# Three chained layers on one core: token blocks of 384 in place of 288, and scores and masks of the first attention pairs formed another way

## The chip, the cores and the metric

One core of a Trainium2 chip runs the kernel. TensorE multiplies matrices into the eight banks of PSUM (b0 to b7), VectorE, ScalarE and GpSimd work element by element, and SyncE (SP) issues the transfers. The metric is the device time of one execution in microseconds.

## The reference

```python
# q, k, v: (4, 8, 576, 64), f: (4, 8, 576)
scores = q @ k^T / 8;  cum = cumsum(log(clip(f, 1e-4, 1)))
scores = where(causal, -1e9, scores + cum[:, None] - cum[None, :])
attn = exp(scores - max) / (sum + 1e-9);  x = attn @ v       # -> (2304 tokens, 512)
h = ((x @ w1) * (x @ w2)) @ w3 @ w_out                       # 512 -> 1024 -> 1024 -> 512
h2 = h @ w_in;  out = (h2 - tanh(h2)) @ w_out2               # 512 -> 2048 -> 512
```

There are 32 heads (4 batches of 8) and 2304 tokens, 576 in a batch.

## The kernel before

**Arithmetic.** A float32 matrix is split into a high part in float32r and the rest, and a product is three float32r products (high by high, high by low, low by high; `mm3`, lines 202 to 205). A weight tile of 128x512 is loaded as 64-bit words into a buffer `w64`, cut to 32 bits by one ScalarE instruction (L279) and four VectorE instructions (L269, L271, L273, L275; `conv`), and split by ScalarE (L289) and GpSimd (L292). A load (L264) waits until VectorE has released a buffer. There are three such buffers (`NW`).

**Attention.** A pair p is two heads (y = 0, 1) of batch p // 4. `head` loads q and k twice, once to the upper and once to the lower 64 partitions (L309), and the row of decays to all partitions (`cumb`, L313). ScalarE casts both (L314, L315: KH, QH), VectorE subtracts (L316: the low part of q in the lower half of QH; L318: KL), and the scores are two float32r products, QH by KH and QH by KL (L325), for pieces of 512, 512, 384, 64, 256 and 128 columns. GpSimd adds the causal mask `tri` (-1e30 above the diagonal) onto the decay row's diagonal block (L331), five times per head. VectorE adds scores and decays, scales them and takes the minimum (L340), ScalarE takes the exponential (L345), TensorE transposes by 128x128 blocks (L386), ScalarE copies them out (L389). The product with the values (`pvm`, L430, and `pvt`, L436) is in float32, 64 output rows per head. The row sums go out and come back by transfer (`dr`, `rb`), and VectorE scales the result into the tile `xy` (L439, L440).

**Layers.** `mphase` forms w3 by w_out once (M, 192 products of 512 columns). `block1` takes 288 tokens through the first layer: the x of the block is cast and subtracted (L482, L483), 16 groups of 12 products with w1 and w2, an elementwise product (L499 to L503), 8 groups of 12 products with M, and the result goes to DRAM (`yd`). A second loop takes the same blocks through the second layer: 16 times 12 products with w_in, eleven elementwise instructions (L601 to L612), 12 products with w_out2. `xy` exists twice, for even and odd batches; blocks 2b and 2b+1 are of batch b.

**Order.** `Plan` collects all operations with engine, estimated length, keys that are read and written, and a due time, and sorts each engine's instructions by a list schedule over these. The due times are lines of the table `PR` with the constants `C`: `att(p)` for pair p (a0, a1 for the first four, a2, a3 for the others), `wo`, `w3`, `w12` for the weight tiles, `m` for M, `blk(t)` for blocks. An engine then runs its list strictly in that order.

## Time and profile before

| | us |
|---|---|
| median of 3 runs (lowest, highest) | 1019.44 (1016.18, 1020.94) |
| the profiled execution | 1024.94 |
| its span from the first to the last instruction | 1023.2 |
| TensorE busy | 950.8 (93%) |
| VectorE busy | 740.0 (72%) |
| ScalarE busy | 604.6 (59%) |
| GpSimd busy | 325.3 (32%) |

The granted TensorE clock is 0.987 on average. Busy time is the share of the span in which an engine has an instruction under way; matmuls overlap one another, so a product's own duration is longer than the distance between two starts.

### The profile page before, as it was taken

How to read it: one execution, taken by the hardware profiler on the slowest of the kernel's cores; microseconds unless marked ns; L12 is line 12 of the kernel's file. 1: busy time of each engine (PE TensorE's matmuls, PEld its weight loads, DVE VectorE, ACT ScalarE, POOL GpSimd, SP SyncE). 2: the span in 40 equal slices, each digit the busy share in tenths (PEclk: the TensorE clock that was granted, in tenths of full speed). 3: DMA queues.
4: the chain of work that ended last, by engine and by line, in shares of the span. 5: the costliest groups of instructions: out<-in, count | busy, mean ns of one | idle time of the engine just before them, and what ended most of it. 6: DMA issues, size and time to landing. Idle time of an engine off the chain costs nothing.

```text
span 1023.2 us, 19522 instructions
## 1 busy us (share of the span) xinstructions
PE 950.8 (93%) x6944; PEld 889.1 (87%) x6944; DVE 740.0 (72%) x1681; ACT 604.6 (59%) x1532; POOL 325.3 (32%) x398
## 2 busy tenths in 40 slices
PE   1788885889999999999999999999999999999998
PEld 1466664778988988899999999999999999999998
DVE  6888898976887868544633238887777777777785
ACT  4766556655656656545422357766666666666674
POOL 1544444431121121110310358424242424242221
PEclk9989999899999999999999999999999999999999
DMA  8556745556677676420410243000000000000000
GB/s 248 168 174 186 199 154 187 151 150 210 200 214 220 186 221 197 117 73 19 137 45 1 76 134 113 24 25 24 24 25 24 24 24 1 24 1 25 1 25 24
DMA packets 46114, 104.25 MB, mean 102 GB/s; under 512 B 5888, under 2 KB 18304, under 8 KB 46016
## 3 DMA queue, kind: packets, MB, share of 16 engines
q1 hardware_dynamic: 46016, 103.01, 33.7%
q8 instruction: 54, 0.88, 0.4%
q14 instruction: 44, 0.36, 0.1%
HBM read 87.11 MB, written 15.88 MB: 101 GB/s over the span
## 4 chain that ended last, share of the span: by engine, by line
PE 65%; DMA 14%; DVE 10%; ACT 6%; issue 3%; SPq 2%; POOL 1%; DVEq 0%; ACTq 0%; POOLq 0%
PE b L205 20%; PE b L204 20%; PE b L203 20%; DMA rb<-dr 5%; DMA spo<-w 3%; PE b L386 2%; DMA cumb<-cumd 2%; PE b L325 2%; DVE w L273 2%; DVE w L275 2%; ACT P L345 1%; DVE w L271 1%; DMA dr<-rt 1%; DVE KL L318 1%; DVE P L340 1%
## 5 line engine op out<-in xcount | busy, mean ns | idle before, releaser
L612 POOL TENSOR_TENSOR gl<-w,gl 128x288 fp32r<-128x288 f32 x120 | 102.5, 854 | 233.6 <-ACT gl L611 230.8
L331 POOL TENSOR_TENSOR cumb<-cumb,tri 128x128 f32<-128x128 f32 (+1 forms) x160 | 89.6, 563 | 272.7 <-DVE MX L340 167.8
L608 ACT ACTIVATE fa<-fa,cb 128x288 f32<-128x288 f32 x128 | 68.6, 536 | 61.2 <-DVE w L607 60.9
L603 DVE SCALAR_TENSOR_TENSOR w<-b,fa 128x288 f32<-128x288 f32 x128 | 57.9, 452 | 60.9 <-ACT fb L602 59.5
L325 PE MATMUL b<-KH,QH 128*64 128x512 f32 (+3 forms) x192 | 68.5, 365 | 32.5 <-DVE MX L340 20.8
L345 ACT ACTIVATE P<-P,MX 128x512 f32<-128x512 f32 (+3 forms) x128 | 71.9, 562 | 23.8 <-DVE MX L340 23.4
L610 DVE COPY_PREDICATED w<-fa,fb 128x288 f32<-128x288 uint32 x128 | 70.0, 547 | 18.9 <-ACT fa L608 10.7
L386 PE MATMUL b<-idf,P 128*128 128x128 f32 x320 | 56.6, 294 | 29.2 <-DVE xy L439 18.2
L607 DVE SCALAR_TENSOR_TENSOR w<-fa,w 128x288 f32<-128x288 f32 x128 | 83.1, 649 | 0.1
L340 DVE CUSTOM_DVE_ANT_0 P<-b,cumb 128x512 f32<-128x512 f32 (+3 forms) x128 | 62.0, 485 | 27.2 <-POOL cumb L331 22.6
L389 ACT COPY PT<-b 128x512 f32<-128x512 f32 (+3 forms) x128 | 51.1, 425 | 51.2 <-PE b L386 49.4
L601 ACT ACTIVATE fa<-b 128x288 f32<-128x288 f32 x128 | 52.5, 410 | 43.1 <-PE b L205 42.9
L386 PEld LDWEIGHTS b<-idf,P 128*128 128x128 f32 x320 | 40.1, 148 | 38.8 <-DVE xy L439 11.2
L325 PEld LDWEIGHTS b<-KH,QH 128*128 128x128 f32 (+1 forms) x192 | 35.0, 182 | 43.5 <-DVE MX L340 26.8
L500 DVE TENSOR_TENSOR fb<-b,fa 128x288 f32<-128x288 f32 x64 | 29.0, 454 | 59.4 <-PE b L205 57.5
L605 ACT ACTIVATE w<-fa,cb 128x288 f32<-128x288 f32 x128 | 69.2, 541 | 0.0
L611 ACT CAST gl<-w 128x288 fp32r<-128x288 f32 x120 | 51.9, 433 | 26.5 <-DVE w L610 26.2
L279 ACT ACTIVATE w<-w 128x512 f32<-128x512 f32 x72 | 48.7, 678 | 31.7 <-DMA spo<-w 8.4
L325 PE MATMUL b<-KL,QH 128*64 128x512 f32 (+3 forms) x192 | 56.9, 336 | 1.1 <-DVE KL L318 1.1
L606 DVE TENSOR_TENSOR fb<-b,fb 128x288 f32<-128x288 f32 x128 | 57.1, 446 | 1.0 <-ACT fb L602 1.0
L273 DVE SCALAR_TENSOR_TENSOR w<-w,w 128x512 uint32<-128x512 uint32 x72 | 55.5, 775 | 0.7
L275 DVE SCALAR_TENSOR_TENSOR w<-w,w 128x512 uint32<-128x512 uint32 x72 | 53.3, 743 | 0.4
(842 smaller groups left out, 3674.1 us busy)
## 6 DMA issues: line engine op xcount, KB each, us to landing
qk<-in_qk_dram SPq DMA_DIRECT2D x64, 288.0 KB
w<-in_wo_dram SPq DMA_DIRECT2D x24, 512.0 KB
cumb<-cumd SPq DMA_DIRECT2D x32, 288.0 KB
w<-in_w3t_dram SPq DMA_DIRECT2D x16, 512.0 KB
...
```

The lines of the kernel that those rows point to most:

```text
L203: E.matmul(o, lh, rh, start=start, stop=False)
L204: E.matmul(o, lh, rl, start=False, stop=False)
L205: E.matmul(o, ll, rh, start=False, stop=stop)
L273: V.scalar_tensor_tensor(m, s[:, :, 1], 0xC0000000, m, ALU.bitwise_and, ALU.bitwise_or)
L275: V.scalar_tensor_tensor(m, s[:, :, 0], 29, m, ALU.logical_shift_right, ALU.bitwise_or)
L325: E.matmul(T[p][0:qn, at:at + c1 - c0], T["QH"][:, 128 * i:128 * i + qn], T[k][:, c0:c1], start=z == 0, stop=z == 1)
L331: G.tensor_tensor(t, t, T["tri"][0:qn, 0:qn], op=ALU.add)
L340: V.tensor_tensor_reduce(out=out, in0=T[p][0:qn, at:at + c1 - c0], in1=T[cum][0:qn, c0:c1], scale=-0.125, scalar=3e38, op0=ALU.add, op1=AL ...
L345: A.activation(t, t, AF.Exp, bias=T["MX"][:, z:z + 1], scale=-1.0, accum_out=T["SM"][:, z:z + 1])
L386: E.transpose(T["b2"][0:n, 128 * z:128 * z + 128], T[src][:, c:c + n], T["idf"])
L607: op("D", d_dve(NB), lambda w=w, u=u: V.scalar_tensor_tensor(T[w], T[u], -P_ROOT, T[w], ALU.add, ALU.mult), r=[u], w=[w], lk=True, **pa)
L612: op("P", d_pool(NB), lambda w=w, gh=gh, gl=gl: G.tensor_sub(T[gl], T[w], T[gh]), r=[w, gh], w=[gl], **pa)
```

## The change

The token block `NB` grows from 288 to 384, so there are 6 blocks in place of 8; three blocks are two batches, and the blocks 1 and 4 reach over the end of a batch. `xy` becomes one tile of two batches' columns with keys for its thirds, `yd` one tensor. The order of declaration is pairs 0 to 3, pairs 4 to 7 with blocks 0 and 1, pairs 8 to 11 with block 2, pairs 12 to 15 with blocks 3 to 5.

For the first five pairs (`nf`) a head's scores are one float32 product of q and k as loaded, over 128 partitions of which the lower 64 are set to zero once; casts, subtractions and the second load are left out. For the first nine pairs (`nm`) the mask is a further small float32r product, an identity (`idr`) by `tri`, added in the same bank; GpSimd's five additions are left out.

The probability tiles P exist once in place of twice, the weight buffers `w64` twice in place of three times, and two scratch tiles come from elsewhere. The constants of the due times all change. The diff, without some lines of the same kind:

```diff
@@ -19,7 +19,7 @@
...
 DM, FF1, FF2 = 512, 1024, 2048
-NB = 288
+NB = 384
 NBLK = NT // NB
...
@@ -35,7 +35,7 @@
...
-C = {"a0": 3.76, "a1": 20.5, "a2": 108.54, "a3": 38.68, "o0": 2.46, "o1": 5.33, "w0": 29.91, "w1": 5.05, "m0": 71.33, "v0": 91.92, "v1": 5.1, "s0": 1170.31, "s1": 10.17, "lod": 2, "evd": 7, "b0": 1619.63, "k0": 1007.92}
+C = {"nf": 5, "nm": 9, "a0": 4.99, "a1": 16.68, "a2": 100.35, "a3": 35.07, "o0": 1.62, "o1": 5.79, "w0": 24.48, "w1": 6.0, "m0": 138.47, "v0": 144.48, "v1": 5.72, "s0": 1192.89, "s1": 8.9, "lod": 1, "evd": 9, "b0": 2090.17, "k0": 1007.92}
 PR = {
...
@@ -47,7 +47,7 @@
...
     "lo_w12": lambda u: "D" if u + 24 < C["lod"] else "P",
-    "blk": lambda t: C["k0"] + 38.1 * t,
+    "blk": lambda t: C["k0"] + 51.0 * t,
     "sp": lambda u: C["s0"] + C["s1"] * u,
...
@@ -308,32 +317,35 @@
...
-        for z in range(2):
+        for z in range(2 if h >= 2 * C["nf"] else 1):
             o("S", 294912, lambda z=z: load(z), t0 - 20, w=[qk, "qk1f"] if y and not z else [f"{qk}.l" if z else qk], pn=64)
         o("S", 294912, lambda: Y.dma_start(T[cum], T["cumd"][h:h + 1].to_broadcast([128, S])), t0 - 8, r=["cumd"], w=ck)
-        o("A", d_act(S, "s"), lambda: A.copy(T["KH"], T[qk][:, 1]), t0 - 6, r=[qk, qk + ".l"], w=["KH"])
-        o("A", d_act(S, "s"), lambda: A.copy(T["QH"], T[qk][:, 0]), t0 - 6, r=[qk, qk + ".l"], w=["QH"])
-        o("D", d_dve(S), lambda: V.tensor_sub(T["QH"][64:128], T[qk][64:128, 0], T["QH"][64:128]), t0 - 6, r=[qk + ".l"], w=["QH"], lk=True)
-        e = PR["lo"](h)
-        o(e, d_dve(S) if e == "D" else d_pool(S), lambda: (V if e == "D" else G).tensor_sub(T["KL"], T[qk][:, 1], T["KH"]), t0 - 6,
-          r=[qk, qk + ".l", "KH"], w=["KL"], lk=True)
+        whole = h < 2 * C["nf"]
+        pem = h < 2 * C["nm"]
+        qks = ["QH", "KH", "KL"] if not whole else [qk, qk + ".l"]
+        if not whole:
+            split(o, t0, h, qk)
...
                 qn = 128 if i < 4 else 64
-                for z, k in enumerate(("KH", "KL")):
-                    E.matmul(T[p][0:qn, at:at + c1 - c0], T["QH"][:, 128 * i:128 * i + qn], T[k][:, c0:c1], start=z == 0, stop=z == 1)
+                qs = slice(128 * i, 128 * i + qn)
+                ops = [(T[qk][:, 0, qs], T[qk][:, 1, c0:c1], 0)] if whole else [(T["QH"][:, qs], T[k][:, c0:c1], 0) for k in ("KH", "KL")]
+                if pem and c1 > 128 * i:
+                    ops.append((T["idr"][0:qn, 0:qn], T["tri"][0:qn, 0:qn], c1 - c0 - qn))
+                for z, (l, r, f) in enumerate(ops):
+                    E.matmul(T[p][0:qn, at + f:at + c1 - c0], l, r, start=z == 0, stop=z == len(ops) - 1)
...
             t = T[cum][0:qn, 128 * i:128 * i + qn]
-            G.tensor_tensor(t, t, T["tri"][0:qn, 0:qn], op=ALU.add)
+            G.tensor_tensor(t, t, T["tri"].bitcast(F32)[0:qn, 0:qn], op=ALU.add)
...
             if i < 4:
-                out, acc = T[f"P{y}{i}"], T["MX"][:, 4 * y + i:4 * y + i + 1]
+                out, acc = T[f"P{i}"], T["MX"][:, 4 * y + i:4 * y + i + 1]
             else:
...
@@ -341,19 +353,19 @@
...
         def sexp(i):
-            t, z = (T[f"P{y}{i}"], 4 * y + i) if i < 4 else (T["J"], 8)
+            t, z = (T[f"P{i}"], 4 * y + i) if i < 4 else (T["J"], 8)
             A.activation(t, t, AF.Exp, bias=T["MX"][:, z:z + 1], scale=-1.0, accum_out=T["SM"][:, z:z + 1])
...
             p = ring("s", SR)
-            du = sum(2 * d_mm(c1 - c0) for i, c0, c1, at in pieces)
-            o("E", du, lambda p=p, pieces=pieces: smm(p, pieces), t, r=["QH", "KH", "KL"], w=[p])
+            du = sum((4 if whole else 2) * d_mm(c1 - c0) + (0.065 if pem and c1 > 128 * i else 0) for i, c0, c1, at in pieces)
+            o("E", du, lambda p=p, pieces=pieces: smm(p, pieces), t, r=qks + (["tri", "idr"] if pem else []), w=[p])
             for i, c0, c1, at in pieces:
                 n = c1 - c0
-                if (i, c0) != (4, 0):
-                    o("P", d_pool(128), lambda i=i: mask(i), t, r=["tri"], w=[ck[i]])
-                k = f"P{y}{i}" if i < 4 else "J"
+                if (i, c0) != (4, 0) and not pem:
+                    o("P", 0.55, lambda i=i: mask(i), t, r=["tri"], w=[ck[i]])
+                k = f"P{i}" if i < 4 else "J"
                 o("D", d_dve(n) + 0.2, lambda p=p, i=i, c0=c0, c1=c1, at=at: smin(p, i, c0, c1, at), t,
...
@@ -375,6 +387,14 @@
...
+    def split(o, t0, h, qk):
+        o("A", d_act(S, "s"), lambda: A.copy(T["KH"], T[qk][:, 1]), t0 - 6, r=[qk, qk + ".l"], w=["KH"])
+        o("A", d_act(S, "s"), lambda: A.copy(T["QH"], T[qk][:, 0]), t0 - 6, r=[qk, qk + ".l"], w=["QH"])
+        o("D", d_dve(S), lambda: V.tensor_sub(T["QH"][64:128], T[qk][64:128, 0], T["QH"][64:128]), t0 - 6, r=[qk + ".l"], w=["QH"], lk=True)
+        e = PR["lo"](h)
+        o(e, d_dve(S) if e == "D" else d_pool(S), lambda: (V if e == "D" else G).tensor_sub(T["KL"], T[qk][:, 1], T["KH"]), t0 - 6,
+          r=[qk, qk + ".l", "KH"], w=["KL"], lk=True)
+
...
@@ -399,8 +419,9 @@
...
         o = lambda e, d, f, z=0.0, **k: op(e, d, f, pr=pt + z, grp="att", **k)
-        xk = f"xy{b % 2}{c}"
-        X = f"xy{b % 2}_{c}"
+        X0 = S * (b % 2)
+        X = lambda: T[f"xy{c}"][:, X0:X0 + S]
+        xk = [[f"xy{c}.{z}" for z in ((0, 1), (1, 2))[b % 2]], [f"xy{c}.{1 + b % 2}"]]
         o("S", 327680, lambda: Y.dma_start(T[VF], a["v"][p]), -12, w=[VF])
...
@@ -436,8 +457,8 @@
...
         o("E", 3.1, lambda: (pvm(), pvt()), 3, r=[VF, "PJ", "PJ4", *[f"PT{y}{i}" for y in range(2) for i in range(4)]], w=["b3", "b2"], mode="c")
-        o("D", d_dve(64), lambda: V.tensor_tensor(T[X][:, 512:576], T["b2"][:, 0:64], T["rb"][:, 512:576], op=ALU.mult), 3.5, r=["b2", "rb0", "rb1"], w=[xk + ".1"])
-        o("D", d_dve(512), lambda: V.tensor_tensor(T[X][:, 0:512], T["b3"], T["rb"][:, 0:512], op=ALU.mult), 3.5, r=["b3", "rb0", "rb1"], w=[xk + ".0", xk + ".1"])
+        o("D", d_dve(64), lambda: V.tensor_tensor(X()[:, 512:576], T["b2"][:, 0:64], T["rb"][:, 512:576], op=ALU.mult), 3.5, r=["b2", "rb0", "rb1"], w=xk[1])
+        o("D", d_dve(512), lambda: V.tensor_tensor(X()[:, 0:512], T["b3"], T["rb"][:, 0:512], op=ALU.mult), 3.5, r=["b3", "rb0", "rb1"], w=xk[0])
...
@@ -471,14 +492,13 @@
...
     def block1(t):
-        b, hf = divmod(t, 2)
-        cols = slice(NB * hf, NB * hf + NB)
+        cols = slice(NB * (t % 3), NB * (t % 3) + NB)
         xk = [(f"xh{c}", f"xl{c}") for c in range(4)]
...
             xh, xl = xk[c]
-            X, src = f"xy{b % 2}_{c}", f"xy{b % 2}{c}.{hf}"
+            X, src = f"xy{c}", f"xy{c}.{t % 3}"
             op("D", d_dve2(NB), lambda xh=xh, X=X: V.tensor_copy(T[xh], T[X][:, cols]), r=[src], w=[xh], pr=t0 - 3, lk=True)
...
@@ -529,12 +549,11 @@
...
     weights12()
-    for b in range(B):
-        if b < 3:
-            for p in range(4 * b + 4, 4 * b + 8):
-                pair(p)
-        for hf in range(2):
-            block1(2 * b + hf)
+    for b, ts in ((1, (0, 1)), (2, (2,)), (3, (3, 4, 5))):
+        for p in range(4 * b, 4 * b + 4):
+            pair(p)
+        for t in ts:
+            block1(t)
     attops = [i for i, o in enumerate(P.ops) if o["grp"] == "att"]
...
@@ -649,29 +666,25 @@
...
     mp = pool(ctx, "main")
-    for b in range(2):
-        for c in range(4):
-            add(mp, f"xy{b}_{c}", [128, S], F32)
+    for c in range(4):
+        add(mp, f"xy{c}", [128, 2 * S], F32)
     add(mp, "cb", [128, 2], F32)
...
         add(mp, n, [128, NB], F32R)
-    for z in range(3):
+    for z in range(2):
         if z < 2:
...
         add(mp, f"w64.{z}", [128, 512, 2], U32)
-        if z == 2:
-            continue
         flat = T[f"w64.{z}"].rearrange("p a b -> p (a b)").bitcast(F32)
-        for y in range(3):
-            T[f"fc{3 * z + y}"] = flat[:, NB * y:NB * y + NB]
+        for y in range(2):
+            T[f"fc{2 * z + y}"] = flat[:, NB * y:NB * y + NB]
     dp = pool(ctx, "scratch", space=DRAM)
...
         add(dp, f"dr{z}", [2, S], F32)
-    for b in range(B):
-        add(dp, f"yd{b}", [4, 128, S], F32)
+    add(dp, "yd", [4, 128, NT], F32)
     for u in range(16):
...
```

## Rows read from the trace of the kernel before

**Rows 1.** Busy time of each engine in stretches of the span, instructions in brackets

```profile
0.00:225.00 225.00, 165.40 (x954) 126.19 (x955) 190.22 (x420) 138.29 (x322) 96.23 (x113) 0.95 0.62 183
225.00:500.00 275.00, 266.15 (x2092) 243.84 (x2091) 188.24 (x528) 156.94 (x432) 51.47 (x97) 0.99 0.55 163
...
615.00:1020.00 405.00, 404.30 (x3039) 404.06 (x3038) 317.71 (x646) 265.66 (x679) 146.87 (x164) 1.00 0.08 25
```

**Rows 2.** Timeline of TensorE, second layer: start us, us, line, operands

```profile
699.70 0.30 PE L205 MATMUL b<-gh,A13l 128*128 128x288 f32 x1
...
701.44 0.29 PE L203 MATMUL b<-gh,A14h 128*128 128x288 f32 x1
```

**Rows 3.** Timeline of TensorE, products of 512 columns

```profile
123.67 0.39 PE L203 MATMUL b<-A0h,A10h 128*128 128x512 f32 x1
...
126.39 0.39 PE L203 MATMUL b<-A4h,A11h 128*128 128x512 f32 x1
```

**Rows 4.** Timeline of TensorE, score products of 384 columns and the next

```profile
105.08 0.34 PE L325 MATMUL b<-KH,QH 128*128 128x384 f32 x1
...
105.42 0.19 PE L325 MATMUL b<-KH,QH 128*64 128x64 f32 x1
...
211.82 0.34 PE L325 MATMUL b<-KH,QH 128*128 128x384 f32 x1
...
212.18 0.19 PE L325 MATMUL b<-KH,QH 128*64 128x64 f32 x1
```

**Rows 5.** Timeline of ScalarE at the span's end

```profile
1019.39 0.40 ACT L627 COPY fa<-b 128x288 f32<-128x288 f32 x1 [0.45 <-PE b L205]
```

**Rows 6.** Groups by line, VectorE, 0 to 225 us: busy, mean ns | idle before

```profile
L273 DVE SCALAR_TENSOR_TENSOR w<-w,w 128x512 uint32<-128x512 uint32 x40 | 33.4, 839 | 0.3
...
L271 DVE TENSOR_SCALAR w<-w 128x512 uint32<-128x512 uint32 x40 | 25.6, 647 | 0.3
...
L318 DVE TENSOR_TENSOR KL<-qk,KH 128x576 fp32r<-128x576 f32 x14 | 13.4, 956 | 2.3 <-ACT KH L314 2.2
...
L316 DVE TENSOR_TENSOR QH<-qk,QH 64x576 fp32r<-64x576 f32 x14 | 12.1, 867 | 0.9 <-ACT QH L315 0.5
```

**Rows 7.** Stretches, L440 alone, the last instruction of a pair (VectorE busy)

```profile
225.00:500.00 275.00, 6.83 (x10) 0.99 0.55 163
```

**Rows 8.** Groups by line and shape, TensorE, whole span

```profile
L430 PE MATMUL b<-PT,VF 128*64 128x512 f32 x64 | 18.2, 647 | 0.0
```

**Rows 9.** Timeline of TensorE, the value product of a pair

```profile
461.78 2.37 PE L430 MATMUL b<-PT,VF 128*64 128x512 f32 x16
```

**Rows 10.** Waits, 0 to 225 us: total, times, longest

```profile
DVE P L340 <- POOL cumb L331: 4.7, 7, 1.5
```

**Rows 11.** Instructions on tile w, 0 to 225 us: min/median/max ns

```profile
L271 DVE TENSOR_SCALAR w<-w x40: 354/422/1981, 11.4 to 208.0; 128x512 uint32<-128x512 uint32 x40
L273 DVE SCALAR_TENSOR_TENSOR w<-w,w x40: 674/684/1779, 11.9 to 208.7; 128x512 uint32<-128x512 uint32 x40
```

**Rows 12.** Timeline of all engines

```profile
114.67 1.72 POOL L292 TENSOR_TENSOR A9l<-w,A9h 128x512 fp32r<-128x512 f32 x1 [1.55 <-ACT A9h L289]
...
115.28 1.72 DVE L318 TENSOR_TENSOR KL<-qk,KH 128x576 fp32r<-128x576 f32 x1
```

**Rows 13.** Groups by line, GpSimd, 0 to 225 us

```profile
L331 POOL TENSOR_TENSOR cumb<-cumb,tri 128x128 f32<-128x128 f32 (+1 forms) x67 | 42.5, 637 | 73.3 <-DVE MX L340 37.2 <-DMA cumb<-cumd 34.5 <-DVE SM L415 1.1
```

**Rows 14.** Timeline of all engines, one weight tile

```profile
129.53 0.33 SPq L264 DMA_DIRECT2D w<-in_w3t_dram  x1
...
133.10 0.68 ACT L279 ACTIVATE w<-w 128x512 f32<-128x512 f32 x1 [0.46 <-DMA w<-in_w3t_dram]
...
136.04 1.28 DVE L275 SCALAR_TENSOR_TENSOR w<-w,w 128x512 uint32<-128x512 uint32 x2
```

**Rows 15.** Stretches, L279 alone, a tile's first instruction (ScalarE busy)

```profile
140.00:212.00 72.00, 10.89 (x16) 0.93 0.57 173
```

**Rows 16.** Waits of the DMA queue SP, 0 to 225 us

```profile
SPq L264 <- DVE w L275: 82.8, 30, 7.0
```

More of the change, by code (lines that the diff above doesn't have):

```diff
@@ L238, in consts @@
     def consts(z):
-        tri, idf = T["tri"], T["idf"]
+        t = T["J"][:, 128 * z:128 * z + 128] if z < 2 else None
         if z == 0:
-            G.memset(idf, 1.0)
-            G.affine_select(idf, idf, pattern=[[1, 128]], compare_op=ALU.is_equal, fill=0.0, base=0, channel_multiplier=-1)
-        else:
-            G.memset(tri, 0.0)
-            G.affine_select(tri, tri, pattern=[[-1, 128]], compare_op=ALU.is_ge, fill=-1e30, base=0, channel_multiplier=1)
-    op("P", 0.8, lambda: consts(1), w=["tri"], pr=-100, grp="att")
-    op("P", 0.6, lambda: consts(0), w=["idf"], pr=-98, grp="att")
+            G.memset(t, 1.0)
+            G.affine_select(t, t, pattern=[[1, 128]], compare_op=ALU.is_equal, fill=0.0, base=0, channel_multiplier=-1)
+        elif z == 1:
+            G.memset(t, 0.0)
+            G.affine_select(t, t, pattern=[[-1, 128]], compare_op=ALU.is_ge, fill=-1e30, base=0, channel_multiplier=1)
+        elif z == 2:
+            V.tensor_copy(T["idr"], T["J"][:, 0:128])
+        elif z == 3:
+            V.tensor_copy(T["tri"], T["J"][:, 128:256])
+        else:
+            G.memset(T[f"qk{z - 4}"][64:128], 0.0)
+    for z in range(2):
+        op("P", 0.7, lambda z=z: consts(z), w=[f"J.{z}", "J"], pr=-100, grp="att")
+        op("D", 0.2, lambda z=z: consts(2 + z), r=[f"J.{z}"], w=["J", ("idr", "tri")[z]], pr=-98, grp="att")
+    for z in range(2):
+        op("P", 1.4, lambda z=z: consts(4 + z), w=[f"qk{z}.l"], pr=-99 + z, grp="att")
     cnt = [0, 0]
     SR = ["b0", "b1"]
-    NW = 3
+    NW = 2
     def conv(unit, hi, lo, pr, spill=None, reload=None, lo_eng="P", grp=None):
@@ L367, in head @@
             if tiles:
-                blocks = [(f"P{y}{i}", 128 * j, 128) for i in tiles for j in range(i + 1)]
+                blocks = [(f"P{i}", 128 * j, 128) for i in tiles for j in range(i + 1)]
                 parts, at = [], 0
@@ L385, in tr @@
             for z, (src, c, n) in enumerate(blocks):
-                E.transpose(T["b2"][0:n, 128 * z:128 * z + 128], T[src][:, c:c + n], T["idf"])
+                E.transpose(T["b2"][0:n, 128 * z:128 * z + 128], T[src][:, c:c + n], T["idr"].bitcast(F32))
         def evac(ev, at, n, rows, out):
             (A.copy if ev == "A" else V.tensor_copy)(out(), T["b2"][0:rows, at:at + n].rearrange("p (a b) -> p a b", b=128))
-        o("E", 0.109 * len(blocks) + 0.02, tr, t, r=["idf", *{x[0] for x in blocks}], w=["b2"])
+        o("E", 0.109 * len(blocks) + 0.02, tr, t, r=["idr", *{x[0] for x in blocks}], w=["b2"])
         for z, (at, n, rows, out, key) in enumerate(parts):
@@ L415, in pair @@
         o("D", 0.12, lambda: V.reciprocal(T["SM"], T["SM"]), 1, w=["SM", *sums])
[L416 removed]
+        o("E", 0.12, lambda: E.transpose(T["b2"][0:9, 0:128], T["SM"], T["idr"].bitcast(F32)), 1, r=["SM", *sums, "idr"], w=["b2"])
         o("A", d_act(128), lambda: A.copy(T["rt"], T["b2"][0:9, 0:128]), 1, r=["b2"], w=["rt"])
@@ L566, in declare @@
     gsl = [(FR[16 + 2 * z], FR[17 + 2 * z]) for z in range(4)]
-    fx = ["fa0", "fa1", "fb0", "fb1"] + [f"fc{z}" for z in range(6)]
+    fx = ["fa0", "fa1", "fb0", "fb1"] + [f"fc{z}" for z in range(4)] + ["yo0", "yo1"]
     usl, tsl, vsl, wsl, osl = fx[0:2], fx[2:4], fx[4:6], fx[6:8], fx[8:10]
@@ L628, in declare @@
                r=[obk[oc]], w=[os_], pr=z - 6)
-            op("S", 147456, lambda os_=os_, oc=oc, t=t: Y.dma_start(a["out"][128 * oc:128 * oc + 128, NB * t:NB * t + NB], T[os_]),
+            op("S", 196608, lambda os_=os_, oc=oc, t=t: Y.dma_start(a["out"][128 * oc:128 * oc + 128, NB * t:NB * t + NB], T[os_]),
                r=[os_], pr=z)
@@ L659, in tile_kernel @@
         add(mp, n, [128, NB], F32R)
-    for z in range(3):
+    for z in range(2):
         if z < 2:
@@ L686, in tile_kernel @@
         add(ap, f"VF{i}", [128, 5, 2, 64], F32)
-        for j in range(4):
-            add(ap, f"P{i}{j}", [128, 128 * j + 128], F32)
+    for j in range(4):
+        add(ap, f"P{j}", [128, 128 * j + 128], F32)
     add(ap, "J", [128, S], F32)
```

13 lines of the change are left out of this document (5 added, 8 removed).

## The prediction

> **What bounds the kernel now.** I read the table of busy time by stage first [rows 1]. From 615 us on TensorE is busy 404.3 of 405 us: the second MoE layer runs at TensorE's own pace. From 225 to 500 us it is busy 266.2 of 275 us, so it nearly sets the pace there too. Before 225 us it is busy only 165.4 us, 59.6 us are left open, and VectorE is the fullest engine with 190.2 us, 85%. So the 1023.2 us of the span are a first stage, in which VectorE prepares 40 weight tiles (four instructions and a load each) while attention runs between, and a dense remainder, in which only TensorE's cost per column counts. A change can gain in two ways: fewer ns per column in the dense part, or an earlier end of the first stage. The profiled execution took 1024.9 us, 5.5 us above the median of 1019.4 us. I sum differences against it and take them off the median.
>
> **Blocks of 384.** Block code issues 288 products per block in the first MoE layer and 384 in the second, for 8 blocks: 5376 of 288 columns. After it is 6 blocks: 4032 of 384 columns. The same columns in fewer instructions; what counts is the fixed part of one. Starts in the dense part: thirteen products of 288 columns between 699.70 and 701.44, 133.8 ns each [rows 2]. Twelve of 512 columns between 123.67 and 126.39, 226.7 ns each [rows 3]. The line through both has 0.4147 ns per column and 14 ns fixed, so 173.6 ns at 384. The score products have that width: two gaps take 0.34 us in one place, 0.36 us in another [rows 4], 175 ns each. Before: 5376 x 133.8 = 719.3 us. After: 4032 x 173.6 = 700.0 us, or 705.6 us with 175. I take -16 us. Bounds: none at all if the cost were proportional (178.4 ns), -25 us if the 0.17 us reading and the rounding of starts both lean my way.
> A rule speaks against this term. The Trainium skill, "TensorE: Matmul & The Clock Gate", section "Back-to-back issue gap", gives columns over 2.4 GHz plus about 2.5 ns, that is, 2.5 ns saved for each of 1344 products that go, 3.4 us in all. The trace disagrees at both widths: 133.8 and 226.7 ns stand where the rule has 122.5 and 215.8 ns. It is a rival below, by the rows alone.
> The elementwise work of a block gets wider in the same proportion, and there are fewer instructions, so VectorE's 317.7 and ScalarE's 265.7 of 405 us [rows 1] fall slightly; neither becomes a bound. The last copy grows with its columns from 0.40 us [rows 5], 0.1 us more.
>
> **Scores of five pairs as one float32 product.** This removes, for ten heads, two ScalarE casts, two VectorE subtractions and half of the q/k load. On VectorE the subtractions L318 and L316 took 0.956 and 0.867 us in the first stage [rows 6]; ten heads make 18.2 us. All five pairs ran in this stage (ten pairs end between 225 and 500 us, so six before [rows 7]), and VectorE limits it: -18 us. Bounds: -21 with the waiting around them, -10 if other waits stand where VectorE was.
> The price is on TensorE. The trace has no full-width float32 score product. The nearest is the product with the values, L430: its 512-column records last 647 ns, two per product [rows 8], against 390 ns for a 512-column float32r record [rows 3]. The excess, 257 ns, is one more pass of 512 columns, so a record is two passes and a product four. Eight products with 64 weight columns (2 x 1280 columns) finish in 2.37 us [rows 9] because the two heads run side by side. A score product with 128 weight columns has no partner: four passes at the line's 0.4147 make 1.66 ns per column, where two float32r products now cost 2 x 226.7/512 = 0.89. A head has 1856 score columns: +1.5 us, 15 us for ten heads. The other bound, two passes, costs nothing more. TensorE has 59.6 us open in the stage, but with 15 us more work in a stage 30 us shorter much of that cover is gone. I take +6; bounds 0 and +15.
>
> **Masks by matmul for nine pairs.** GpSimd loses 5 masks for each of 18 heads; TensorE gains as many products of 128 columns (one of 64) in a group that is open anyway, 14 + 128 x 0.4147 = 67 ns, 6.0 us together. Those of some three pairs fall in the dense part: +2 us; bounds 0 and +6. VectorE no longer waits for a mask: 4.7 us in the first stage [rows 10]. I take -3, since the load of the decay row may be late next; bounds 0 and -5.
> The larger effect is on VectorE's own durations. L273 has a median of 0.684 and L271 of 0.422 us [rows 11], but means of 0.839 and 0.647 in this stage [rows 6]; maxima reach 1.8 and 2.0 us. The stretch on these two lines is 40 x (0.155 + 0.225) = 15.2 us. At 115.28 a subtraction L318 takes 1.72 us, against its mean of 0.956, and GpSimd's L292 runs from 114.67 for 1.72 us [rows 12]. So VectorE stretches while GpSimd works. Masks are 42.5 [rows 13] of GpSimd's 96.2 us in the stage [rows 1], 44%; of 15.2 us that is 6.7 us, and with a part for the two other lines of a conversion I take -10; bounds 0 and -30, the stretch of all four doubled up.
> The Trainium skill, "SBUF — State Buffer", section "SBUF: two separate sides", names the cause: GpSimd and a VectorE instruction that uses the second read port exclude each other for a whole instruction. The trace agrees with 1.72 us against 1.72 us. By that rule the whole term would be the time that masks and such instructions overlap, at most the 42.5 us of masks.
>
> **What the room for the blocks costs.** The weight buffers go from three to two. A load issued at 129.53 is used at 133.10, 3.6 us; its conversion ends at 136.04 + 1.28, 4.2 us later [rows 14]. With two buffers a tile can come every (3.6 + 4.2)/2 = 3.9 us. Between 140 and 212 us 16 tiles came in 72 us, 4.5 us each [rows 15], and a stage shorter by 30 us wants all 40 at about 4.8. So it just fits. But behind a load that waits for its buffer, all other loads queue on SP: L264 waited 82.8 us there [rows 16], with the decay rows, q/k and the reciprocal sums behind it. +5; bounds 0 and +20. One set of P tiles and one double-wide x set: a head's exponentials must wait until the head before has been transposed, and batch 2 until blocks 0 and 1 have copied their x. A pair takes 27.5 us (275 us for ten [rows 7]), far more than such a tile is held, and x is copied at a block's start. Of the first five pairs q and k are held to the last score product, no longer than the decay row beside them already is: +3, bounds 0 and +10.
>
> **The order.** The instructions are sorted by due times, and these move too. Before, the last weight tile is due at 91.92 + 15 x 5.1 = 168, after pair 5 (147); now at 230, after pair 7 (205). Two pairs more come before the dense part and two fewer within it. That shifts work from one side of the boundary to the other and changes neither sum, so I price it at nothing; but the boundary itself may then stay near 225 us, and the gain show as fewer open us on TensorE. With the loads, masks and copies that move along, the queues keep their lengths.
>
> **Sum.** -16 + 0.1 - 18 + 6 + 2 - 3 - 10 + 5 + 3 = -31 us. 1024.9 - 31 = 994 us as the profile counts, 988 us on the median. All of the first-stage gain (31 us before its costs) fits into TensorE's 59.6 open us.
>
> **Rivals.**
> 1. Two weight buffers pace the first stage. For it: the 82.8 us of waiting with three. Against it: 3.9 us possible, 4.8 wanted. If loads behind one another put a tile at 5.6 us, 40 tiles end where they end now, the first-stage gain is gone, and what remains is -16 + 2 = 1005 us (1000 to 1014).
> 2. The dense part gains only 2.5 ns per product. For it: nothing in rows 2 and 3, unless 384 columns fall off their line; two of the four gaps at 384 allow 0.18 us, no gain. Then 988 + 13 = 1001 us, and the starts would lie 177 ns apart or more.
> 3. Slower: attention of the last eight pairs falls behind the blocks. Before, two blocks of the batch already finished run while the next batch's pairs do; after, block 1 straddles batches 0 and 1 and block 4 batches 2 and 3. From the start of block 2 (when batch 3 may write x) until block 4 needs batch 3, TensorE has blocks 2 and 3, 2 x 288 x 0.1736 = 100 us, and four pairs. A pair costs it 2.4 us with the values, 2 x 1.65 in scores (1856 x 0.89 ns) and at least 26 x 0.067 in transposes, 7.4 us: 130 us in all, so 32 us per pair. At the present 27.5 us [rows 7] it fits by 20 us. Beyond 32 us per pair every us costs 4, in two places (batch 2 before block 3 likewise). To end above 1024.5 it must eat 36 us, which needs some 37 us per pair.
>
> **How the numbers follow.** Forecast 0.62 (own range 970 to 1003), two buffers 0.20, no gain per column 0.07, late attention 0.11. The range 966 to 1012 leaves out the slow rival's 0.11, the top of the first (0.04) and the tails of the forecast (0.05). A difference of 0.5%, 5 us, is about what a measurement of this kernel tells from none. Slower by more: 0.09 of rival 3. Within: 0.02 of it and 0.04 of rival 1. Faster: 0.85.
>
> **What would show it.** In the second layer products of 384 columns start 173 to 176 ns apart. In the first stage VectorE has twenty subtractions fewer, L273 and L271 means near 0.75 and 0.5 us, and no wait for masks in pairs 0 to 8. The float32 scores show two records per product, 512 columns every 0.85 us. TensorE's open time before it becomes dense falls from 60 us to 30. I am wrong if the gaps are 178 ns, if the last of the 40 tiles comes as late as now, or if TensorE idles in the middle before block 1 or 4.

## The result, and the profile after

The changed kernel takes 991.5 us (median of 4; 988.4 to 995.5), against 1020.0 us for the kernel before in the runs beside it: a ratio of 0.972, 95% interval 0.969 to 0.975. It is 28.5 us faster; the forecast was 31 us, 988 us. Its profiled execution took 991.8 us with a span of 990.1 us.

The total came out nearly as forecast, but not from the terms of the sum. First the table of stages of the changed kernel, with the columns of [rows 1]: TensorE, weight loads, VectorE, ScalarE, GpSimd, granted clock, DMA share, GB/s.

```profile
0.00:225.00 225.00, 202.70 (x1186) 149.27 (x1187) 182.10 (x460) 148.31 (x365) 57.13 (x49) 0.95 0.61 186
225.00:500.00 275.00, 267.58 (x1754) 245.82 (x1753) 184.49 (x466) 143.79 (x364) 49.41 (x77) 1.00 0.51 157
500.00:586.00 86.00, 86.00 (x489) 86.00 (x488) 26.09 (x44) 33.57 (x68) 30.31 (x25) 1.00 0.28 84
586.00:987.00 401.00, 400.39 (x2267) 400.06 (x2265) 290.97 (x482) 239.35 (x506) 133.95 (x122) 1.00 0.07 21
```

Before 225 us TensorE is open for 22.3 us instead of 59.6, and GpSimd works 57 us instead of 96. From 225 to 500 us little changes: 7.4 us open against 8.9. Over the whole span TensorE is busy 956.7 us, before 950.8: it was not relieved, it waits less. Up to 500 us it is open 29.7 us instead of 68.5.

Next TensorE's timeline in the second layer, where [rows 2] stood before, and then the first product of two blocks, four blocks apart.

```profile
700.20 0.34 PE L204 MATMUL b<-gh,A14h 128*128 128x384 f32 x1
...
702.32 0.34 PE L204 MATMUL b<-gl,M3h 128*128 128x384 f32 x1
...
640.67 0.34 PE L203 MATMUL b<-gh,B0h 128*128 128x384 f32 x1
...
912.03 0.34 PE L203 MATMUL b<-gh,B0h 128*128 128x384 f32 x1
```

Twelve steps take 2.12 us, 176.7 ns each. The blocks come every (912.03 - 640.67)/4 = 67.84 us, over 384 products 176.7 ns again. The forecast had 173.6 to 175 ns. The same reading of the kernel before, over six blocks:

```profile
656.76 0.30 PE L203 MATMUL b<-gh,B0h 128*128 128x288 f32 x1
...
963.26 0.29 PE L203 MATMUL b<-gh,B0h 128*128 128x288 f32 x1
```

51.08 us per block, 133.0 ns per product. So all products of the layers went from 5376 x 133.03 = 715.2 us to 4032 x 176.67 = 712.3 us: 2.9 us, not 16.

VectorE in the first 225 us of the changed kernel (busy, mean ns, idle before; L280 and L282 are the lines that were L271 and L273 in [rows 6], L278 and L284 the two other lines of a conversion, L269 and L275 before):

```profile
L284 DVE SCALAR_TENSOR_TENSOR w<-w,w 128x512 uint32<-128x512 uint32 x40 | 31.2, 782 | 0.5
L282 DVE SCALAR_TENSOR_TENSOR w<-w,w 128x512 uint32<-128x512 uint32 x40 | 30.7, 772 | 0.2
L280 DVE TENSOR_SCALAR w<-w 128x512 uint32<-128x512 uint32 x40 | 20.4, 515 | 0.5
L278 DVE TENSOR_SCALAR w<-w 128x512 f32<-128x512 f32 x41 | 20.0, 489 | 17.6 <-ACT w L288 17.2
...
L395 DVE TENSOR_TENSOR KL<-qk,KH 128x576 fp32r<-128x576 f32 x8 | 7.0, 880 | 2.4 <-ACT KH L391 2.3
L393 DVE TENSOR_TENSOR QH<-qk,QH 64x576 fp32r<-64x576 f32 x8 | 6.0, 756 | 0.6 <-ACT QH L392 0.3
```

The conversions are less stretched, 0.772 and 0.515 us against 0.839 and 0.647, as forecast (0.75 and 0.5). The subtractions that remain are those of pairs 5 to 8. VectorE's wait for a mask [rows 10] is gone.

The last of the 40 weight tiles does not come earlier, as the sum supposed. Its cast on ScalarE, before and after:

```profile
211.33 0.62 ACT L289 CAST A7h<-w 128x512 fp32r<-128x512 f32 x1 [1.07 <-DVE w L275]
```

```profile
222.94 0.62 ACT L298 CAST A7h<-w 128x512 fp32r<-128x512 f32 x1 [0.80 <-DVE w L284]
```

It comes 11.6 us later.

Last, when the pairs end. The last instruction of a pair is L440 before and L461 after; the row has min/median/max ns, then first and last start. Before:

```profile
L440 DVE TENSOR_TENSOR xy<-b,rb x16: 679/684/692, 53.6 to 491.4; 128x512 f32<-128x512 f32 x16
...
278.42 0.68 DVE L440 TENSOR_TENSOR xy<-b,rb 128x512 f32<-128x512 f32 x1
...
1019.00 0.30 PE L205 MATMUL b<-xl,M7l 128*128 128x288 f32 x1
```

After:

```profile
L461 DVE TENSOR_TENSOR xy<-b,rb x16: 676/682/692, 44.3 to 474.4; 128x512 f32<-128x512 f32 x16
...
220.11 0.68 DVE L461 TENSOR_TENSOR xy<-b,rb 128x512 f32<-128x512 f32 x1
...
986.05 0.34 PE L205 MATMUL b<-xl,M7l 128*128 128x384 f32 x1
```

The single rows are pair 7 and the last product of all. Pair 7 ends 58 us earlier, the last pair only 17 us earlier: the pairs between them take (474.4 - 220.1)/8 = 31.8 us each, before 26.6. And from the last pair to the last product 511.6 us are left, before 527.6.

Where TensorE still waits in the changed kernel, and on what: first its waits from 225 to 500 us (total, times, longest), then the stretch from 420 us to the last product.

```profile
PE b L406 <- DVE xy L460: 3.8, 5, 1.1
PE b L406 <- ACT PJ L409: 1.5, 1, 1.5
PE b L406 <- ACT PT L409: 1.2, 2, 0.9
PE b L337 <- DVE MX L352: 0.9, 1, 0.9
```

```profile
420.00:986.00 566.00, 566.00 (x3263) 561.83 (x3262) 358.68 (x618) 307.06 (x656) 179.29 (x162) 1.00 0.12 37
```

The four waits make up all of the 7.4 us. L406 (transposes) and L337 (scores) are instructions of a pair, so wherever TensorE is open in this stretch, a pair holds it. Half of it ends with L460, which reads the bank b2 that the next transposes write. From 420 us on TensorE is never open: it does not wait for the last pair.

### The profile page after: what moved, and what is told of

It is laid out like the page before. It is cut to its first block, busy times and chain, and to the rows that moved or that the text cites. A ratio compares the mean times of both kernels' runs of the same rounds, so it can differ in the third digit from the quotient of the medians.

```text
span 990.1 us, 16118 instructions
## 1 busy us (share of the span) xinstructions
PE 956.7 (97%) x5690; PEld 881.1 (89%) x5690; DVE 683.6 (69%) x1450; ACT 565.0 (57%) x1300; POOL 270.8 (27%) x271
## 3 DMA queue, kind: packets, MB, share of 16 engines
q1 hardware_dynamic: 41760, 100.05, 32.9%
## 4 chain that ended last, share of the span: by engine, by line
PE 76%; DMA 10%; ACT 5%; DVE 4%; issue 2%; SPq 1%; POOL 0%; ACTq 0%; DVEq 0%; POOLq 0%
PE b L203 22%; PE b L204 22%; PE b L205 22%; PE b L337 5%; DMA rb<-dr 4%; PE b L406 4%; DMA w<-in_wo_dram 2%; DMA w<-in_win_dram 1%; ACT P L357 1%; ACT w L288 1%; DVE w L282 1%; PE b L451 1%; DMA w<-in_w3t_dram 1%; DMA w<-in_w_dram 1%; DVE w L284 1%
## 5 line engine op out<-in xcount | busy, mean ns | idle before, releaser
L629 POOL TENSOR_TENSOR gl<-w,gl 128x384 fp32r<-128x384 f32 x88 | 93.1, 1058 | 247.5 <-ACT gl L628 245.7
L620 DVE SCALAR_TENSOR_TENSOR w<-b,fa 128x384 f32<-128x384 f32 x96 | 53.2, 554 | 98.3 <-ACT fb L619 98.2
L625 ACT ACTIVATE fa<-fa,cb 128x384 f32<-128x384 f32 x96 | 59.3, 617 | 88.3 <-DVE w L624 88.3
L357 ACT ACTIVATE P<-P,MX 128x256 f32<-128x256 f32 (+3 forms) x128 | 71.5, 561 | 6.9 <-DVE MX L352 6.1
L624 DVE SCALAR_TENSOR_TENSOR w<-fa,w 128x384 f32<-128x384 f32 x96 | 74.6, 778 | 0.0
L626 DVE SCALAR_TENSOR_TENSOR w<-w,w 128x384 f32<-128x384 f32 x96 | 67.6, 705 | 8.4
L352 DVE CUSTOM_DVE_ANT_0 P<-b,cumb 128x128 f32<-128x128 f32 (+3 forms) x128 | 61.0, 485 | 16.4 <-PE b L406 7.9
L627 DVE COPY_PREDICATED w<-fa,fb 128x384 f32<-128x384 uint32 x96 | 64.7, 674 | 9.3 <-ACT fa L625 1.6
L628 ACT CAST gl<-w 128x384 fp32r<-128x384 f32 x88 | 45.0, 512 | 38.3 <-DVE w L627 38.3
L406 PE MATMUL b<-idr,P 128*128 128x128 f32 x320 | 54.0, 284 | 11.9 <-DVE xy L460 9.1
L406 PEld LDWEIGHTS b<-idr,P 128*128 128x128 f32 x320 | 39.4, 144 | 26.1 <-DVE xy L460 7.3
L337 PE MATMUL b<-qk 128*64 128x512 f32 (+5 forms) x120 | 48.1, 498 | 13.3 <-DVE MX L352 8.0
L278 DVE TENSOR_SCALAR w<-w 128x512 f32<-128x512 f32 x72 | 33.6, 466 | 38.1 <-ACT w L288 37.6
L622 ACT ACTIVATE w<-fa,cb 128x384 f32<-128x384 f32 x96 | 59.1, 615 | 0.0
L284 DVE SCALAR_TENSOR_TENSOR w<-w,w 128x512 uint32<-128x512 uint32 x72 | 54.6, 759 | 0.8
L282 DVE SCALAR_TENSOR_TENSOR w<-w,w 128x512 uint32<-128x512 uint32 x72 | 53.9, 751 | 0.7
```

The source lines that it names most:

```text
L282: V.scalar_tensor_tensor(m, s[:, :, 1], 0xC0000000, m, ALU.bitwise_and, ALU.bitwise_or)
L284: V.scalar_tensor_tensor(m, s[:, :, 0], 29, m, ALU.logical_shift_right, ALU.bitwise_or)
L337: E.matmul(T[p][0:qn, at + f:at + c1 - c0], l, r, start=z == 0, stop=z == len(ops) - 1)
L357: A.activation(t, t, AF.Exp, bias=T["MX"][:, z:z + 1], scale=-1.0, accum_out=T["SM"][:, z:z + 1])
L406: E.transpose(T["b2"][0:n, 128 * z:128 * z + 128], T[src][:, c:c + n], T["idr"].bitcast(F32))
L624: op("D", d_dve(NB), lambda w=w, u=u: V.scalar_tensor_tensor(T[w], T[u], -P_ROOT, T[w], ALU.add, ALU.mult), r=[u], w=[w], lk=True, **pa)
```

## The experiments

In the first runs one theory was that of the sum (its terms each worth what it says), one that the new due times make the gain, one that two weight buffers take much of it back. The ratios below are to the kernel before, run on the same chip; a difference between two ratios is given in us at 1020 us.

**The blocks without the attention parts.** The changed kernel, with both counts of pairs at zero; buffers and due times as after.

```
- C = {"nf": 5, "nm": 9, ...
+ C = {"nf": 0, "nm": 0, ...
```

> The changed kernel with both attention parts switched off (nf = 0, nm = 0): blocks of 384, two weight buffers and the new due times stay, all 32 heads go by casts, subtractions and GpSimd masks. First theory (the prediction's sum): the blocks give 16 us, their room costs 8, so 1004 to 1014 us, faster than before. Second theory (read from the profile after: the second layer takes 67.84 us per 384 tokens and took 51.08 per 288, so a product of 384 columns costs 176.7 ns and the blocks give 3 us): 1015 to 1030, not faster. Third theory (the new due times make the gain): 990 to 1000.

Measured 1.010 (1.006 to 1.013), 1032 us: 1% slower than before, and above the ranges of all three theories; the second, at 1015 to 1030, is the nearest. In this run the granted clock before 225 us is 0.89 on average, in the kernel before 0.95, so a part of the loss is products at the lower of the two clocks; how much is not shown.

**The attention parts without the blocks.** The kernel before with the new attention code; 288 tokens, three buffers and the old due times stay.

```
+ C = {"nf": 5, "nm": 9, "a0": 3.76, "a1": 20.5, ...
```

> The kernel before with only the attention parts (float32 scores for five pairs, masks by matmul for nine); blocks of 288, three weight buffers, two sets of P and the old due times stay. First theory: 18 + 10 + 3 - 6 - 2 = 23 us, so about 997, with the loss of buffers not paid. Second theory: nearly all of the 28 us come from here, 990 to 996. Third theory (due times): 1012 to 1020, since the order was made for other lengths.

Measured 0.980 (0.975 to 0.984), 1005 us: a smaller gain than the first and the second theory have, a larger one than the third.

**The same with the new due times.** The one above with the changed kernel's line of constants.

> The same as the run with the attention parts alone, but with the changed kernel's due times (the steps between blocks stay those of 288 tokens). First theory: about 997, as without them. Second theory: 985 to 995, as the changed kernel, since the blocks bring 3 us and their room costs about as much. Third theory: at least 10 us below the run with the old due times.

Measured 0.986 (0.982 to 0.990), 1010 us: none of the three theories.

**The due times alone.** The kernel before with that line of constants, and nothing else.

> The kernel before with nothing but the constants of the due times of the changed kernel. First and second theory: 1012 to 1030, no gain. Third theory (the due times make the gain): 990 to 1000.

Measured 1.007 (1.004 to 1.010), 1030 us. The new due times cost 7 us here, and 6 us beside the attention parts, where the intervals overlap; they gain in neither, so the third theory falls. If they cost as much with blocks of 384, some 7 of the 10 us that blocks, buffers and due times lose without the attention parts are theirs.

**Each attention part taken away.** The changed kernel without the masks by matmul ("nm": 0), and without the float32 scores ("nf": 0).

> The changed kernel with the masks of all pairs by GpSimd again (nm = 0); float32 scores for five pairs stay. The prediction priced the masks by matmul at 10 + 3 - 2 = 11 us, mostly as less stretch of VectorE's instructions: 1000 to 1006 us, a ratio of 0.98 to 0.985 to the kernel before, and the means of the conversion lines back near 0.84 and 0.65 us. Rival: the stretch costs VectorE nothing on the path, 990 to 995.

> The changed kernel with casts, subtractions and two float32r products for all heads (nf = 0); masks by matmul for nine pairs stay. The prediction priced the float32 scores at 18 - 6 = 12 us: 1000 to 1008 us, ratio 0.98 to 0.99. Rival: TensorE pays for them as much as VectorE saves (15 us more products), so 988 to 995.

Measured 0.9915 (0.989 to 0.994) without the masks and 0.991 (0.989 to 0.993) without the float32 scores. So the masks are worth 19.7 us and the scores 19.2, at 1020 us times the difference in ratio to 0.972; together 38.9, and both taken away at once lose (1.0097 - 0.9722) x 1020 = 38.3. They add up, and each is worth more than the sum has (11 and 12 us) and than either expectation allowed. VectorE's lines without the masks by matmul, 0 to 225 us:

```profile
L282 DVE SCALAR_TENSOR_TENSOR w<-w,w 128x512 uint32<-128x512 uint32 x37 | 30.8, 831 | 0.3
...
L284 DVE SCALAR_TENSOR_TENSOR w<-w,w 128x512 uint32<-128x512 uint32 x36 | 25.9, 720 | 0.3
L280 DVE TENSOR_SCALAR w<-w 128x512 uint32<-128x512 uint32 x37 | 24.3, 657 | 0.2
L278 DVE TENSOR_SCALAR w<-w 128x512 f32<-128x512 f32 x37 | 17.8, 482 | 16.8 <-ACT w L288 16.4
```

On L282 and L280 the stretch is back, at 0.831 and 0.657 us; on L284 and L278 it is not, 0.720 and 0.482 us. Over the four lines a conversion takes 132 ns more than in the changed kernel, 5.3 us for 40 tiles, of the 19.7. Pair 7 ends 23 us later, at 243.5, the last pair 25 us later, and the last weight tile is cast at 244.8 us, 22 us later. What makes these 20 us and more out of the 5 is not shown; GpSimd, which forms the low part of the weight tiles too, works 100 us before 225 us in place of 57.

**Two weight buffers, 288 tokens.** The attention parts with the new due times, and two buffers in place of three.

```
-     NW = 3
+     NW = 2
```

> The run with the attention parts, blocks of 288 and the changed kernel's due times (1009.9 us, 0.9856), with two weight buffers in place of three. The prediction priced the lost buffer at 5 us, with bounds 0 and 20: 1010 to 1020. If two buffers set the pace of the tiles, 1020 or more. If they cost nothing, 1008 to 1011, and the blocks of 384 are what makes the step from 0.9856 to 0.9722.

Measured 0.989 (0.985 to 0.992): 3 us more than with three buffers, with intervals that overlap, though the last weight tile is cast at 229.9 us in place of 214.5. From here to the changed kernel only the block size and the buffers it shares memory with are left (with the steps between their due times), and that step is worth (0.9888 - 0.9722) x 1020 = 17 us, though the products become only 2.9 us cheaper. TensorE from 150 to 225 us, in this kernel and in the changed one:

```profile
150.00:225.00 75.00, 65.71 (x463) 54.06 (x464) 65.11 (x148) 50.39 (x126) 19.21 (x14) 0.95 0.63 181
```

```profile
150.00:225.00 75.00, 74.13 (x496) 63.94 (x495) 69.14 (x158) 54.78 (x132) 20.32 (x15) 1.00 0.62 189
```

9.3 us open against 0.9, at a granted clock of 0.95 against 1.00. A tile that arrives brings block 0 work of 384 columns in place of 288, 12 products each: 2.12 us instead of 1.60.

**The fixed part of a product, by itself.** Appended to the changed kernel, in one execution: bursts of 96 products into one sum, of several widths, first with a weight tile as the moving operand (A0h), then with an x tile (xh0).

```
+ for mov, n in (("A0h", 512), ("A0h", 384), ("A0h", 288), ("A0h", 192), ("A0h", 128), ("xh0", 384), ...):
+     for z in range(96):
+         E.matmul(T["b0"][:, 0:n], T[f"A{1 + z % 7}h"][:, 0:128], T[mov][:, 0:n], start=z == 0, stop=z == 95)
```

> The changed kernel, followed at its end by bursts of 96 products each whose results nobody reads: a weight tile as the moving operand with 512, 384, 288, 192 and 128 columns, then an x tile with 384, 288 and 192. First theory (a line with 14 ns fixed and 0.4147 ns per column): 227, 174, 133, 94 and 67 ns. Second theory (proportional, as 176.7 and 133.0 ns in the second layer suggest, 0.460 ns per column): 236, 177, 133, 88 and 59 ns. A fixed 2.5 ns over 2.4 GHz: 216, 163, 123, 83 and 56 ns. If only the place of the moving operand matters, the weight tile's bursts lie on the first line and the x tile's on the second.

TensorE's timeline, first and last product at 384 columns, then at the end of the burst of 192:

```profile
1010.06 0.33 PE L654 MATMUL b<-A0h,A1h 128*128 128x384 f32 x1
...
1026.55 0.33 PE L654 MATMUL b<-A0h,A5h 128*128 128x384 f32 x1
...
1041.80 0.27 PE L654 MATMUL b<-A0h,A2h 128*128 128x192 f32 x1
...
1043.92 0.27 PE L654 MATMUL b<-A0h,A7h 128*128 128x192 f32 x1
```

95 steps in 16.49 us, 173.6 ns: in a burst 384 columns lie on the forecast's line, and so do 512 (226.7 ns) and, within 2 ns, 288 (131.7 where the line has 133.8). The x tile takes 173.9 ns at 384 columns and 133.3 at 288, so the place of the moving operand does not make 176.7. Below the line lies a floor, which none of the expected lines had: at 192 columns 19 steps take 2.12 us, 111.6 ns, and 128 columns take as long.

**Streams like the layers'.** Also appended, in one execution: 96 products in eight sums of 12, over three banks, with nine choices of operands and order (seven at 384 columns, two at 288).

> The changed kernel, followed by streams of 96 products of 384 columns whose results nobody reads, in eight groups of 12 over three banks: one x tile with changing weight tiles; with the eight x tiles in turn; with the four slices of the weight tiles; with high and low weight tiles in turn; then the order of the layers (high-high, high-low, low-high for each of four slices); the order high-high, low-high, high-low; and all high-high before all high-low before all low-high; then the layers' order and the second one with 288 columns. The burst before gave 173.7 ns, the layers run at 176.7. If the order or the operands cost the 3 ns, the layers' order shows 176 to 177 and the first stream 173 to 174, and one of the others names the cause; if all lie at 173 to 174, what costs is the work of the other engines or the waits between groups, not the operands.

```profile
999.94 0.34 PE L670 MATMUL b<-xh,A4h 128*128 128x384 f32 x1
...
1002.06 0.34 PE L670 MATMUL b<-xh,A0h 128*128 128x384 f32 x1
```

Twelve steps in 2.12 us: 176.7 ns, in all seven, and 133.3 ns at 288. Neither answer that was expected came: the first stream already has what the layers have. So neither the order of high and low parts, nor the choice among these operands, nor other engines' work makes the 3 ns. At 288 columns the burst with the x tile has the streams' 133.3 ns already; at 384 columns 2.8 ns remain between its 173.9 and the streams. What still differs there is one sum on one bank against eight sums on three, and which weight tiles take turns; that stays open.

**Work taken from block 0, and from block 2.** The products that feed on the w1 and w2 tiles run on 288 of a block's 384 columns, so the sums of 96 columns of its first layer are left out: 192 products x 43.7 ns = 8.4 us of TensorE.

```
-  mm3(bk(p), T[wh][:, sl], T[wl][:, sl], T[xk[kc][0]], T[xk[kc][1]], kc == 0, kc == 3)
+  n = 288 if t == 0 else NB
+  mm3(T[p][:, 0:n], T[wh][:, sl], T[wl][:, sl], T[xk[kc][0]][:, 0:n], T[xk[kc][1]][:, 0:n], kc == 0, kc == 3)
```

In block 0:

> The changed kernel in which the products of block 0 with w1 and w2 are made for 288 of its 384 tokens only (the other 96 columns of those sums are left out); the order of all instructions is the same. That takes 192 x (176.7 - 133.0) = 8.4 us from TensorE at the time when the last weight tiles arrive. Theory: the larger block 0 fills time in which TensorE would wait for the next tile, 1.6 us of work per group becoming 2.1; taking it away opens that time again and saves little, 0 to 4 us: ratio 0.968 to 0.973 to the kernel before. Rival: TensorE is the bound there too, so the 8.4 us come off: 0.962 to 0.965.

In block 2 (t == 2):

> The same products left out of block 2, which lies in the dense part. Both theories: TensorE is the bound, so the 8.4 us come off, ratio 0.962 to 0.966. If it is no faster than the run with block 0 cut, the cut of block 0 says nothing about waiting.

Measured 0.973 (0.971 to 0.976) and 0.9735 (0.971 to 0.976): neither gains anything on 0.972. For block 0 the open time from 150 to 225 us rises from 0.9 to 8.5 us. For block 2 the expectations missed: there, where TensorE seemed full, it opens as well. From 300 to 400 us, with block 2 cut and then in the changed kernel:

```profile
300.00:400.00 100.00, 86.83 (x596) 78.09 (x595) 73.55 (x189) 52.06 (x135) 16.58 (x30) 0.95 0.62 185
```

```profile
300.00:400.00 100.00, 95.16 (x628) 86.08 (x627) 74.24 (x192) 53.79 (x137) 17.60 (x31) 1.00 0.65 199
```

8.3 us more are open there, as much as the 8.4 that were taken away; up to 500 us it is 38.1 us, and 38.3 with block 0 cut, against 29.7. In this stretch the granted clock fell too, from 1.00 to 0.95, so the products that were left took longer; with block 0 cut the clock before 225 us is 0.95 as in the changed kernel, and the result is the same. The waits in which TensorE opens, with block 2 cut, 300 to 400 us:

```profile
PE b L406 <- ACT PJ L409: 4.9, 2, 2.6
PE b L406 <- DVE xy L460: 4.6, 3, 3.1
PE b L406 <- ACT PT L409: 2.1, 1, 2.1
PE b L337 <- DVE MX L352: 1.6, 1, 1.6
```

They are all of the 13.2 us, and all are a pair's. The last pair, with block 2 cut:

```profile
L461 DVE TENSOR_TENSOR xy<-b,rb x16: 678/684/693, 43.3 to 478.3; 128x512 f32<-128x512 f32 x16
```

It ends no earlier. A TensorE that is busy 95% of a stretch didn't set its pace: the pairs did.

**Late weight loads taken away.** What holds the pairs? The waits of the changed kernel from 225 to 475 us (total, times, longest), cut to those of VectorE and ScalarE for DMAs:

```profile
DVE xy L460 <- DMA rb<-dr: 24.7, 7, 14.6
...
ACT w L288 <- DMA w<-in_wo_dram: 15.0, 10, 3.4
...
ACT w L288 <- DMA w<-in_win_dram: 5.0, 5, 1.9
```

VectorE's wait at L460 is for the row sums on their way back; 14.6 of its 24.7 us are in the last pair, where TensorE has other work. ScalarE, which also computes the pairs' exponentials, waits for a weight tile fifteen times. With two buffers such a load can start only when the tile two before it is converted. In the next kernel the 24 tiles that are converted here and stored for the second layer are loaded with an eighth of their columns (the rest of these weights is left out); the instructions stay.

```
- Y.dma_start(T[k64], unit...)
+ n = 512 if spill is None else 64
+ Y.dma_start(T[k64][:, 0:n], unit...[:, 0:n])
```

> The changed kernel in which the 24 weight tiles that are converted between the pairs and put back to memory for the second layer are loaded with an eighth of their columns (the rest of each buffer is old); order and all other instructions are the same. In the changed kernel ScalarE waits 20 us between 225 and 475 us for these loads, behind which the pairs' own instructions stand; a pair takes 31.8 us there, and the end comes 511.7 us after the last pair. Theory (two weight buffers, whose loads come late, pace the pairs in the middle): the waits go, a pair takes 30.5 us or less, and 6 to 9 us come off, no more, since TensorE has only 9 us open after 225 us: ratio 0.963 to 0.967. Rival (TensorE's own list and the pairs' chain pace the middle): less than 2 us, ratio 0.970 to 0.973.

Measured 0.966 (0.963 to 0.969), 985 us: 6.7 us less than the changed kernel. Stage and last pair:

```profile
225.00:500.00 275.00, 273.19 (x1791) 253.36 (x1791) 187.62 (x467) 144.32 (x367) 50.59 (x78) 1.00 0.40 119
...
L462 DVE TENSOR_TENSOR xy<-b,rb x16: 678/684/693, 42.8 to 464.7; 128x512 f32<-128x512 f32 x16
```

TensorE is open 1.8 us in the stage instead of 7.4, ScalarE's waits for those two weights fall from 20 us to 2.5, and the last pair ends 9.7 us earlier (the line number has moved by one; the profiled execution is the fastest of six, 3 us below their median). The wait for the row sums hardly changes, 22.5 us; GpSimd's for the decay rows falls from 55.6 to 46.7. The thinner loads also take traffic off the transfers, 119 GB/s in place of 157; that this helps the pairs by itself is not excluded. What else sets the 31.8 us of a pair stays open.

## Why the total was right and the terms were not

**Where the time went.** The prediction took the end as a first stage, which ends with the 40th weight tile, plus TensorE's dense remainder. Read as TensorE's busy and open time, the change is 5.9 us more work (956.7 against 950.8) and 38.8 us less open time (29.7 against 68.5): -32.9 of the -33.1 us between the spans. The sum had -7.9 us for TensorE's work (-16, +0.1, +6 and +2) and -23 us for the waits (-18, -3, -10, +5 and +3). So the total is near by luck: the work came out 14 us worse and the waits 16 us better.

The end of the first stage did not come earlier either: the 40th tile comes 11.6 us later. The prediction names that as a sign of being wrong, and for its picture of the stage it was. What ended earlier are the first pairs, pair 7 by 58 us, and TensorE found work in what was open time.

What holds TensorE, where it is open after 225 us, are the pairs: all 7.4 us of its waits there are theirs, the two cuts of its work gained nothing, and the thinner loads, which let the pairs run faster, brought 6.7 us. After 420 us it holds itself, by the work that its list has left. That is also why six of the kernels with 384 columns, the changed one among them, have 511 to 512 us after their last pair, whether that starts its last instruction at 464.7 or at 499.4 us (519 in the seventh, without either attention part): the list has the same work behind it. This number alone shows no bound.

It does show that little room is left. Block 4 straddles batches 2 and 3, so when the last pair ends, two blocks of the first layer and six of the second must still come: 2 x 288 x 176.7 ns = 101.8, and 6 x 67.84 = 407.0, together 508.8 of the 511.6 us. In the kernel before, two first-layer blocks and eight of the second were 76.6 + 408.6 = 485.3 us, and 527.6 were left: 42.3 us of work that did not need the last pair. In the changed kernel it is 2.8 us, so a last pair that ended some 3 us later would hold TensorE too. That is worked out from these rows; no run tests it.

**Blocks of 384: -16 forecast, -2.9 measured.** The failed step is "so 173.6 ns at 384": a line through 288 columns in the layers and 512 columns in a short stretch of the first stage. The line is real in bursts. In the layers it is 133.0 and 176.7 ns, nearly proportional (177.4 would be). The 176.7 lies between the 176 that the prediction wanted to see and the 178 that it named as a sign of being wrong. The size of the term is near that of rival 2 (3.4 us), but by another way than a fixed 2.5 ns per product. The Trainium skill, "TensorE: Matmul & The Clock Gate", section "Back-to-back issue gap", gives these 2.5 ns on top of columns at 2.4 GHz for the gap of a product taken by itself, not for a stream. The streams here have 12 to 14 ns on top in the bursts (226.7, 173.6 and 131.7 ns against 213.3, 160.0 and 120.0) and 13 to 17 in the layers.

**The attention parts: -23 forecast (the terms -18, +6, +2, -3 and -10), -38.9 measured.** The wait for masks went. The four lines of a conversion together fell by 9.7 us over 40 tiles (forecast 10), but only 5.3 us of it come back with the masks, so about half of it has another cause. The float32 product fits four passes, as argued. TensorE's timeline in the changed kernel, a product with 64 weight columns, one with 128 and its mask, and the next ones:

```profile
96.56 1.07 PE L337 MATMUL b<-qk 128*64 128x512 f32 x2
97.56 0.50 PE L203 MATMUL b<-A1h,A12h 128*128 128x512 f32 x1
...
98.79 1.02 PE L337 MATMUL b<-qk 128*128 128x512 f32 x2
99.25 0.62 PE L337 MATMUL b<-tri,idr 128*128 128x128 f32 x1
99.71 0.45 PE L203 MATMUL b<-A2h,A12h 128*128 128x512 f32 x1
```

Two records each; 1.00 us to the next product, and 0.92 us with the mask in it, which leaves 0.85 us with the mask at the forecast's 0.067, or 0.81 with the 0.111 us that 128 columns took in the bursts. Without the float32 scores TensorE is busy 9.7 us less (947.0 us, at a granted clock of 0.93 before 225 us against 0.95), between the +6 taken and the 15 that were its bound. What was mis-sized is what VectorE's microseconds are worth. They were counted one for one, as in a stage that VectorE fills; but VectorE's work also lies in the pairs' chain, and without the masks by matmul pair 7 ends 23 us later, not 11. Why by so much is not shown. In the kernel of 288 the same parts give 20 us only; there the last pair ends earlier too, at 454.0, but 546 us are left after it.

**Two buffers: +5 forecast in the first stage.** With 288 tokens 3 us, within the intervals; in the changed kernel their late loads cost up to 6.7 us, but from 225 to 500 us. The size was right, the place not. Rival 1's condition came true, 40 tiles that end no earlier than before, and with 288 tokens two buffers put the last one 15.4 us later; but its price, 1005 us, did not follow, since the last tile is not what the end waits for.

**The order, priced at nothing.** Its paragraph comes nearest to the outcome: the boundary stays near 225 us, and the gain shows as pairs done early and TensorE less open. Its price was not nothing, some 6 us in the kernels of 288. A part of the 17 us of the last step pays it back: block 0's wider products fill TensorE's open time while tiles arrive (9.3 to 0.9 us), which the sum has nowhere. How much of the 17 us this is, is argued, not shown: with 384 columns the pairs also wait for one another in other places.

**Rival 3, late attention.** It needed more than 32 us per pair. The pairs took 31.8 us, where the argument had 27.5, so the slack of 20 us is used up. By that argument the change stands at the edge of this rival; no run goes beyond it.

So the sum was right by luck, because its errors cancel: 13 us too much on the blocks, 16 too little on the attention parts, and 6 us or so of due times unpriced.
